# Decode block on one core: the second MLP layer with batches on four column groups, folded into rows of 512 bytes, and a first MLP layer that finishes eight column tiles early

## The chip, the core and the metric

The kernel runs on one core of a Trainium2 chip. The metric is the device time of one execution in microseconds (us). Times within the profile ("at 663.3") count from the first instruction; the span from the first to the last instruction is some 1.7 to 1.8 us shorter than the device time.

In the profile's lines PE is TensorE's matmuls, PEld its weight loads, DVE VectorE, ACT ScalarE, SPq and ACTq the issue of a transfer by the sync and the scalar engine. A transfer has *landed* when the last of its completions is counted. A *column group* is 32 of the array's 128 columns, worked as a small array of its own.

## The reference

One decode step of a block with adaptive layer norm: modulation from `c`, cached attention over 8192 keys, then an MLP with squared ReLU. What matters here is its last line and the MLP:

```python
# B = 8 batches, D = 512, F = 1792; k_cache and v_cache are (8, 8, 8192, 128) bf16
mod = silu(c) @ w_mod                       # six vectors of 512 per batch
x = x + ga * attention(h, k_cache, v_cache, wq, wo)
h = layernorm(x) * (1 + cb) + sb
r = maximum(h @ w1 + b1, 0)
x = x + gb * ((r * r) @ w2 + b2)            # the part that the change rewrites
```

## The kernel before

Nearly everything is loaded through one queue, the sync engine's: `w_mod`, `wq`, then 64 units of keys and values of 4 MB each through four ring slots, and at the very end, in the ring slot that came free, W1 in two pieces and W2 in four:

```python
d_w1 = [dma("sync", s_w1[i], ...W1v[:, a:z]...) for i, (a, z) in enumerate(((0, 3), (3, 4)))]
d_w2 = [dma("sync", s_w2[i], ...W2v[:, a:z, :]...)
        for i, (a, z, j) in enumerate(((0, 4, 4), (4, 8, 4), (8, 12, 4), (12, 14, 2)))]
```

The MLP keeps hidden units on partitions and the 8 batches in the columns. The first layer walks k outermost over all 14 column tiles, so no tile is complete before the last k. The second layer loads each 128x128 block of W2 as the stationary operand and streams 8 columns. Its result has the output features on partitions, so it must be transposed through TensorE before it can be stored:

```python
for f in range(FT):                          # FT = 14 row tiles of W2
    for k in range(KT):                      # KT = 4 column blocks
        t = op("tensor", lambda e: e.matmul(yT_ps[:, k, :], W2v[:, f, k*128:(k+1)*128], hidT[:, f, :],
               ...), [k_sq[f // 8], d_w2[f // 4]])      # waits for the piece of W2
...                                          # residual x1T transposed into o_ps (L778)
k_y2 = op("vector", ... y2T = yT_ps * mod(5))           # L781
for cc in (1, 0):
    ...                                      # y2T transposed into o_ps (L786)
    # copy o_ps to SBUF on ScalarE (cc = 1) or VectorE (cc = 0), then store 8 rows of 512 bytes
```

Of the kernel before, what the change touches and what calls it, by code (L numbers as in the profile page):

```python
# [5 lines left out]
ACT = mybir.ActivationFunctionType  # L6
ALU = mybir.AluOpType
# [161 lines left out]
def bass_adaLN_cond__gqa_block_cached__dense_activation_squared_relu__decode_kernel(  # L169
# [17 lines left out]
    with ExitStack() as es:  # L187
# [25 lines left out]
        SEL = sb("SEL", [128, 4, 8], BF16)  # L213
# [13 lines left out]
        SELB = sb("SELB", [4, 4, B], BF16)  # L227
        SELP = sb("SELP", [128, B], FP32)
        x1T = sb("x1T", [128, KT, B], BF16)
# [4 lines left out]

        KF = KTb[:, :, :, :].rearrange("p a t r -> p (a t r)")
# [10 lines left out]
        EYEB = KF[:, 4544:4576].rearrange("p (g b) -> p g b", g=4)  # L246
# [5 lines left out]
        hidT = KF[:, 2560:2560 + FT * B].rearrange("p (f b) -> p f b", f=FT)  # L252
        out_sb = KF[:, 2048:2304]
# [4 lines left out]
        y2T = KF[:, 0:KT * B].rearrange("p (k b) -> p k b", k=KT)  # L258
# [34 lines left out]
        def pool(fn, deps=()):  # L293
            return op("gpsimd", fn, deps)

        pool(lambda e: e.memset(IDENT[:], 0.0))
        pool(lambda e: e.memset(IDF8[:], 0.0))
# [4 lines left out]
        pool(lambda e: e.memset(R4m[:], 0.0))  # L302
        pool(lambda e: e.memset(SEL[:], 0.0))
# [6 lines left out]
        def select(ap, pattern, base, cm, fill, cmp, dep):  # L310
            return pool(lambda e: e.affine_select(ap, ap, pattern=pattern, compare_op=cmp, fill=fill,
                                                  base=base, channel_multiplier=cm), [dep])
# [3 lines left out]
        t = select(IDF8[:], [[-1, 8]], 0, 1, 1.0, NE, t)  # L316
        k_id = t
        pool(lambda e: e.memset(KF[:, 4096:4096 + 64 * KT], 0.0))
        pool(lambda e: e.memset(EYE[:], 0.0))
        t = pool(lambda e: e.memset(EYEB[:], 0.0))  # L320
        t = select(EYE[:], [[-32, 4], [-1, B]], 0, 1, 1.0, NE, t)
        t = k_eye = select(EYEB[:], [[-32, 4], [-1, B]], 0, 1, 1.0, NE, t)
# [3 lines left out]
        for d in (-96, -64, -32, 0, 32, 64, 96):  # L326
            t = select(R4[:], [[-1, 128]], -d, 1, 1.0, NE, t)
        t = select(Qmask[:], [[-32, 4]], 0, 1, 0.0, GE, t)
        t = select(Qmask[:], [[32, 4]], 31, -1, 0.0, GE, t)
        for d in (0, 32, 64, 96):  # L330
            t = select(R4m[:], [[-1, 32]], -d, 1, 0.5, NE, t)

        for i in range(4):
            for cg in range(4):
                for half in range(2):
                    t = select(SEL[:, i, 4 * half:4 * half + 4], [[-1, 4]], -(32 * cg + 8 * i + 4 * half), 1,
                               1.0, NE, t)
# [5 lines left out]
        t = select(SELB[:], [[-1, 4], [0, B]], 0, 1, 1.0, NE, t)  # L343
# [89 lines left out]
        for u in range(2):  # L433
            for i in range(4):
                t = op("tensor", lambda e, u=u, i=i: e.matmul(
                    QT_ps[:, u, :, i, :], q_r[:, u, DH * i:DH * (i + 1)], EYEB[:, :, :]), [k_q[u]])
# [12 lines left out]
        k_cb1 = op("vector", lambda e: e.tensor_scalar(cb1[:], mod(4), 1.0, None, ALU.add))  # L449

# [8 lines left out]
        d_bb = dma("sync", s_bb, lambda e: e.dma_start(b2_row, B_b2.rearrange("(o f) -> o f", o=4)))  # L459
# [57 lines left out]
        yT_ps = bank(2)[:, 0:KT * B].rearrange("p (k b) -> p k b", k=KT)  # L517
# [31 lines left out]
        for b in range(B):  # L549
# [76 lines left out]
            for p in range(NP):  # L626
# [22 lines left out]
                if not lastu:  # L649
# [9 lines left out]
                    for i in range(4):  # L659
                        t = op("tensor", lambda e, i=i, osb=osb, oT_ps=oT_ps: e.matmul(  # L660
                            oT_ps, osb[:, i * 128:(i + 1) * 128], SEL[:, i, :], start=(i == 0), stop=(i == 3)),
                            [k_osb, k_all])
                        if i == 0:
                            released[n % NSLOT] = t
                            if n + NSLOT < len(units):
                                load(n + NSLOT)
# [7 lines left out]
                else:  # L674
# [29 lines left out]
                    for hh, (f0, n, a, z) in enumerate(((0, 4, 0, 2), (0, 4, 2, 3), (4, 2, 3, 4))):  # L704
                        for j in range(n):
                            op("tensor", lambda e, hh=min(hh, 1), f0=f0 + j, j=j, n=n, a=a, z=z: e.matmul(
                                hT_ps[hh][:, f0:f0 + 4 * (z - a - 1) + 1:4, 1, :], brow(j, n), SELB[:, a:z, :],
                                start=(f0 == 0), stop=False, skip_group_check=True), [d_bb, s_bank_free[min(hh, 1)]])
                    op("tensor", lambda e: e.matmul(
                        yT_ps, b2_row, SELB[:, :, :], start=True, stop=False, skip_group_check=True),  # L710
# [6 lines left out]
                    for i in range(4):  # L717
                        op("tensor", lambda e, i=i: e.matmul(
                            oT_ps, osb[:, i * 128:(i + 1) * 128], SEL[:, i, :], start=False, stop=False,
                            skip_group_check=True), [t, k_all])  # L720
# [16 lines left out]
        k_x1 = op("vector", lambda e: e.tensor_tensor(x1T[:], t1T[:], xT[:], ALU.add), [t])  # L737
        mean_ps = bank(3)[:, 0:B]
        for k in range(KT):
            t = op("tensor", lambda e, k=k: e.matmul(mean_ps, ONESMB[:, :], x1T[:, k, :], start=(k == 0),  # L740
                                                    stop=(k == KT - 1)), [k_x1])
        bc = lambda ap: ap.unsqueeze(1).to_broadcast([128, KT, B])
        t = op("vector", lambda e: e.tensor_tensor(xcT[:], x1T[:], bc(mean_ps), ALU.subtract), [t])
# [8 lines left out]
        for k in range(KT):  # L752
            if k == KT - 1:
                t = op("tensor", lambda e: e.matmul(var_ps, ONESM[:, :], sqs[:]), [k_sqs])
                t = op("scalar", lambda e: e.activation(std2[:], var_ps, ACT.Sqrt, bias=epst[:, 0:1]), [t])
                k_rstd = op("vector", lambda e: e.reciprocal(rstd2[:], std2[:]), [t])
            for f in range(FT):
                t = op("tensor", lambda e, f=f, k=k: e.matmul(
                    hT_ps[f // 8][:, f % 8, :, :], wcol(k, f), hbT[:, k, :, :], start=False, stop=(k == KT - 1),
                    skip_group_check=True), [k_hb, k_sb, d_w1[k // (KT - 1)]])  # L760
                if k == KT - 1 and f in (7, FT - 1):
                    hh = f // 8
                    fs = slice(8 * hh, f + 1)
                    t = op("vector", lambda e, hh=hh, fs=fs: e.tensor_tensor(
                        rT[:, fs, :], hT_ps[hh][:, :, 0, :], rsb(fs.stop - fs.start), ALU.mult), [t, k_rstd])
                    t = op("vector", lambda e, hh=hh, fs=fs: e.tensor_tensor(
                        rT[:, fs, :], rT[:, fs, :], hT_ps[hh][:, :, 1, :], ALU.add), [t])
                    k_sq.append(op("vector", lambda e, fs=fs: e.scalar_tensor_tensor(
                        hidT[:, fs, :], rT[:, fs, :], 0.0, rT[:, fs, :], ALU.max, ALU.mult), [t]))
        o_ps = bank(4)[:, 0:256]  # L770
        for f in range(FT):
            for k in range(KT):
                t = op("tensor", lambda e, f=f, k=k: e.matmul(  # L773
                    yT_ps[:, k, :], W2v[:, f, k * 128:(k + 1) * 128], hidT[:, f, :],
                    start=False, stop=(f == FT - 1), skip_group_check=True), [k_sq[f // 8], d_w2[f // 4]])
        for cc in range(2):
            for k in range(2):
                op("tensor", lambda e, k=k, cc=cc: e.matmul(  # L778
                    o_ps[64 * cc:64 * cc + B, 128 * k:128 * (k + 1)], x1T[:, 2 * cc + k, :], IDENT[:, :],
                    start=(k == 0), stop=False, tile_position=(0, 64 * cc), skip_group_check=True), [k_x1])  # L780
        k_y2 = op("vector", lambda e: e.tensor_tensor(y2T, yT_ps, mod(5), ALU.mult), [t])  # L781
        outf = out.rearrange("b s d -> (b s) d")
        d_o = []
        for cc in (1, 0):
            for k in range(2):
                t = op("tensor", lambda e, k=k, cc=cc: e.matmul(  # L786
                    o_ps[64 * cc:64 * cc + B, 128 * k:128 * (k + 1)], y2T[:, 2 * cc + k, :], IDENT[:, :],
                    start=False, stop=(k == 1), tile_position=(0, 64 * cc), skip_group_check=True), [k_y2])
            rows = slice(64 * cc, 64 * cc + B)
            if cc == 0:  # L790
                t = op("vector", lambda e, rows=rows: e.tensor_copy(out_sb[rows, :], o_ps[rows, :]), [t])
            else:
                t = op("scalar", lambda e, rows=rows: e.activation(out_sb[rows, :], o_ps[rows, :], ACT.Copy), [t])
            d_o.append(dma(("sync", "scalar")[cc], s_out[cc], lambda e, cc=cc, rows=rows: e.dma_start(
                outf[:, 256 * cc:256 * (cc + 1)], out_sb[rows, :]), [t]))
# [32 lines left out]
```

## Time and profile before

| | before |
|---|---|
| time, median of 3 | 668.38 us (668.37 to 668.46) |
| span in the profile | 666.7 us |
| moved by the 16 DMA engines | 283.85 MB at 426 GB/s |
| TensorE / VectorE / ScalarE busy | 79% / 46% / 40% |
| granted TensorE clock from 658 us on | 0.50 |

The busy shares say little: TensorE is busy 79% of the span, and yet the DMA engines are above 90% busy in every slice but the last, so there is little to win before the last few microseconds. The reader has to look at the tail by itself. Here are the two output issues, from the timeline of the kernel before (start, length, engine):

```profile
664.85 0.30 ACTq L794 DMA_DIRECT2D out_dram<-KTb  x1
664.92 0.31 SPq L794 DMA_DIRECT2D out_dram<-KTb  x1
```

### The profile page before, as it was taken

To read this page: it belongs to the slowest core of one execution; us is meant where nothing else is said; L and a number is where in the kernel's file an instruction comes from. 1 tells how busy PE (TensorE), PEld (TensorE's weight loads), DVE (VectorE), ACT (ScalarE), POOL (GpSimd) and SP (SyncE) were. 2 spreads that over 40 slices of the span, in tenths; PEclk is the share of its full clock that TensorE was granted. 3 is DMA by queue.
4 is the path that set the end of the run, shared out by engine and by line. 5 is a ranking of instruction groups with operands and counts; after the bars stand their busy time and mean duration, and the time that the engine had idled before them with its cause. 6 is when DMAs were issued, how large, how long until landed. Compare 5 with 4: busy or idle time off the path is not lost.

```text
span 666.7 us, 15924 instructions
## 1 busy us (share of the span) xinstructions
PE 528.3 (79%) x7259; PEld 352.2 (53%) x7259; DVE 307.9 (46%) x587; ACT 264.3 (40%) x307; POOL 20.5 (3%) x79
## 2 busy tenths in 40 slices
PE   3494976898849987599858988499776998589887
PEld 2383732675328742477316753287424773277535
DVE  1262741466316652367415662167513673146633
ACT  2151631466115651166314661166512663146611
POOL 7400000000000000000000000000000000000000
PEclk9696998799969999699998999799997999879996
DMA  9999999999999999999999999999999999999997
GB/s 375 437 406 441 419 433 433 425 434 431 438 427 433 433 434 427 434 434 425 434 431 438 427 431 434 434 427 431 438 425 434 433 436 427 431 434 434 427 420 285
DMA packets 12189, 283.85 MB, mean 426 GB/s; under 512 B 1261, under 2 KB 1297, under 8 KB 3601
## 3 DMA queue, kind: packets, MB, share of 16 engines
q1 hardware_dynamic: 12128, 283.65, 99.3%
q8 instruction: 9, 0.15, 0.1%
q10 hardware_dynamic: 48, 0.02, 0.0%
q14 instruction: 4, 0.02, 0.0%
HBM read 283.66 MB, written 0.01 MB: 425 GB/s over the span
## 4 chain that ended last, share of the span: by engine, by line
PE 52%; DMA 38%; ACT 6%; DVE 2%; issue 1%; SPq 0%; DVEq 0%
PE PS L488 36%; DMA ring<-in_A_k_cache_dram 33%; PE PS L505 9%; ACT P_sb L582 5%; DMA ring<-in_A_v_cache_dram 4%; DMA ring<-in_A_wq_dram 2%; PE PS L636 2%; PE PS L478 1%; ACT KTb L493 1%; DVE O_sb L656 1%; PE PS L472 1%; PE PS L594 1%; DVE Pm L608 0%; PE PS L614 0%; PE PS L773 0%
## 5 line engine op out<-in xcount | busy, mean ns | idle before, releaser
L488 PE MATMUL PS<-IDENT,ring 128*128 128x128 bf16 x4096 | 267.1, 227 | 56.2 <-DMA ring<-in_A_k_cache_dram 56.2
L488 PEld LDWEIGHTS PS<-IDENT,ring 128*128 128x128 bf16 x4096 | 246.5, 102 | 104.8 <-DMA ring<-in_A_k_cache_dram 57.4
L493 ACT ACTIVATE KTb<-PS 128x1024 bf16<-128x1024 bf16 x192 | 196.5, 1024 | 236.6 <-PE PS L488 236.6
L495 DVE COPY KTb<-PS 128x1024 bf16<-128x1024 bf16 x320 | 210.0, 688 | 146.5 <-PE PS L488 144.4
L636 PE MATMUL PS<-ring,Pm 128*32 128x512 bf16 x1018 | 67.2, 409 | 24.8 <-DMA ring<-in_A_v_cache_dram 23.9
L505 PE MATMUL PS<-KTb,Qb 128*32 128x512 bf16 x1024 | 79.0, 385 | 4.5 <-ACT KTb L493 4.5
L656 DVE CAST O_sb<-PS 128x512 bf16<-128x512 f32 x31 | 21.5, 692 | 112.7 <-PE PS L636 112.7
L636 PEld LDWEIGHTS PS<-ring,Pm 128*32 128x32 bf16 x1018 | 26.5, 101 | 61.8 <-DMA ring<-in_A_v_cache_dram 33.7
L535 ACT ACTIVATE KTb<-PS 32x192 bf16<-32x192 f32 (+1 forms) x18 | 5.6, 310 | 110.0 <-PE PS L472 103.9
L582 ACT ACTIVATE P_sb<-PS,negm 128x1024 bf16<-128x1024 f32 x32 | 35.2, 1111 | 20.2 <-DVE negm L577 20.2
L478 PE MATMUL PS<-ONES 128*128 128x512 f32 x80 | 42.1, 630 | 0.0
L472 PE MATMUL PS<-IDENT 128*128 128x512 bf16 x112 | 33.4, 380 | 0.0
L594 PE MATMUL PS<-IDENT,P_sb 128*128 128x128 bf16 x256 | 19.9, 220 | 15.4 <-ACT P_sb L582 15.4
L608 DVE COPY Pm<-PS 64x512 bf16<-64x512 bf16 x48 | 20.2, 421 | 25.0 <-PE PS L594 24.5
L594 PEld LDWEIGHTS PS<-IDENT,P_sb 128*128 128x128 bf16 x256 | 14.4, 98 | 25.1 <-ACT P_sb L582 25.1
L505 PEld LDWEIGHTS PS<-KTb,Qb 128*32 128x32 bf16 x1024 | 15.4, 94 | 21.0 <-ACT KTb L493 8.5
L512 DVE TENSOR_REDUCE m<-PS 128x1 f32<-128x512 f32 x32 | 22.1, 689 | 6.6 <-PE PS L505 6.6
L660 PEld LDWEIGHTS PS<-SEL,O_sb 128*128 128x128 bf16 x124 | 5.8, 97 | 30.0 <-DVE O_sb L656 30.0
L478 PEld LDWEIGHTS PS<-ONES 128*128 128x128 f32 x80 | 12.7, 190 | 10.6 <-issue 10.6
L660 PE MATMUL PS<-SEL,O_sb 128*128 128x8 bf16 x124 | 7.8, 169 | 12.3 <-DVE O_sb L656 12.0
L472 PEld LDWEIGHTS PS<-IDENT 128*128 128x128 bf16 x112 | 9.9, 104 | 10.1 <-issue 7.2
L543 PE MATMUL PS<-wo_sb,KTb 128*32 128x512 bf16 x192 | 11.8, 380 | 3.3 <-ACT KTb L535 3.3
(134 smaller groups left out, 147.0 us busy)
## 6 DMA issues: line engine op xcount, KB each, us to landing
ring<-in_A_k_cache_dram SPq DMA_DIRECT2D x32, 4096.0 KB, 34.0
ring<-in_A_v_cache_dram SPq DMA_DIRECT2D x31, 4096.0 KB, 27.8
ring<-in_A_wq_dram SPq DMA_DIRECT2D x1, 4096.0 KB, 19.8
wo_sb<-in_A_wo_dram SPq DMA_DIRECT2D x1, 4096.0 KB, 47.3
ring<-in_w_mod_dram SPq DMA_DIRECT2D x1, 3072.0 KB, 10.5
ring<-in_A_v_cache_dram SPq DMA_DIRECT2D x1, 2048.0 KB, 22.5
ring<-in_B_w_dram SPq DMA_DIRECT2D x3, 512.0 KB, 19.2
ring<-in_B_w_dram SPq DMA_DIRECT2D x1, 1344.0 KB, 17.8
```

The source lines that it names most:

```text
L472: ts = [op("tensor", lambda e: e.matmul(bank(at).rearrange("p (a r) -> p a r", a=4), IDENT[:, :], rhs)) for _ in range(n)]
L478: ts = [op("tensor", lambda e: e.matmul(bank(at).rearrange("p (a r) -> p a r", a=4), ONES[:, :], rhs)) for _ in range(n)]
L488: t = op("tensor", lambda e, j=j, i=i: e.matmul(STG[j][:, i, :], src[:, 32 * k + 8 * j + i, :], IDENT[:, :], is_transpose=True), [loaded[n ...
L493: stg_free[j] = op("scalar", lambda e, j=j, dst=dst: e.activation(dst, STG[j], ACT.Copy), [t])
L495: stg_free[j] = op("vector", lambda e, j=j, dst=dst: e.tensor_copy(dst, STG[j]), [t])
L505: t = op("tensor", lambda e, hf=hf, q=q, rhs=rhs: e.matmul(PS[32 * q:32 * (q + 1), k, :], Qb[:, 2 * p + hf, :], rhs, start=(p == 0 and hf ...
L512: return op("vector", lambda e: e.tensor_reduce(m4[:, k:k + 1], bank(k), AX.X, ALU.max), [t])
L582: exps.append(op("scalar", lambda e, k=k: e.activation(P_sb[:, k, :, :, :], bank(k).rearrange("p (i x) -> p i x", i=8).unsqueeze(2).to_bro ...
L594: t = op("tensor", lambda e, k=k, i=i: e.matmul(STG[k][:, i, :], P_sb[:, k, i, :, :].rearrange("p h x -> p (h x)"), IDENT[:, :], is_transp ...
L608: done.append(op("vector", lambda e, dst=dst, frm=frm: e.tensor_copy(dst, frm), [t, k_pm]))
L636: t = op("tensor", lambda e, m=m, cg=cg, p=p, vt=vt, Obank=Obank: e.matmul(Obank[32 * cg:32 * (cg + 1), :], lhs[:, p, 32 * m:32 * m + 32], ...
L656: t = op("vector", lambda e, osb=osb, Obank=Obank: e.tensor_copy(osb, Obank), [t])
```

## The change

Its intent is to shorten that tail in three places. The first layer runs column tiles 0 to 7 for all four k before tiles 8 to 13, so that eight tiles of the hidden layer are ready early, and the variance matmul moves forward with it. The second layer puts the batches (8, padded to 32) into the stationary operand and streams 128 columns of W2, on four column groups of the array at once. Its result then has batches on partitions and needs no transpose: one multiply by the gate, two adds that fold 128 partitions into 64, and the store. The core of the diff:

```diff
-        for k in range(KT):
-            if k == KT - 1: ... variance, sqrt, reciprocal
-            for f in range(FT): ... first layer
+        for hh, (fa, fz) in enumerate(((0, 8), (8, FT))):
+            for k in range(KT):
+                if (hh, k) == (0, 2): ... variance, sqrt, reciprocal
+                for f in range(fa, fz): ... first layer
...
         for f in range(FT):
             for k in range(KT):
-                    yT_ps[:, k, :], W2v[:, f, k * 128:(k + 1) * 128], hidT[:, f, :],
+                    y_ps[32 * k:32 * (k + 1), :], hidw[:, f, :], W2v[:, f, 128 * BLK[k]:128 * (BLK[k] + 1)],
+                    ... tile_position=(0, 32 * k)
...
-        k_y2 = ... y2T = yT_ps * mod(5);  transposes of x1T and y2T into o_ps;  two copies
+        t = op("vector", lambda e: e.tensor_tensor(y_sb, y_ps, mod5[:], ALU.mult), [t])
+        for h in range(2):
+            rows = slice(64 * h, 64 * (h + 1))
+            t2 = op("vector", lambda e, h=h, rows=rows: e.tensor_tensor(
+                out_sb[:, h, :], y_sb[rows, :], x1_sb[rows, :], ALU.add), [t, k_res])
```

The rest prepares this: `hidw` and `x1w` are zero-padded to 32 columns, `mod5` holds the gate in the new layout, x1 is brought into it early (L739, L769).

## The prediction

> **What bounds the kernel now.** I read the page first: the slices and the chain.
>
> ```profile
> span 666.7 us, 15924 instructions
> ...
> DMA  9999999999999999999999999999999999999997
> ...
> q1 hardware_dynamic: 12128, 283.65, 99.3%
> ```
>
> The 16 DMA engines are above 90% busy in every slice but the last. What they move (283.65 MB in that queue) is untouched by the change, so at most the last slice or so can be won. That is the tail: the second MLP half and the output, after the last values have landed. The chain of waits in order of time, cut to that stretch (start, length, what):
>
> ```profile
> 658.28 1.53 PE PS L758 x42
> 659.80 0.44 PE PS L754 x2
> 660.25 0.02 issue
> 660.27 0.28 ACT std L755
> ...
> 661.40 0.24 DVE KTb L768
> 661.64 0.04 issue
> 661.68 1.02 PE PS L773 x32
> 662.70 0.13 issue
> 662.83 0.92 PE PS L773 x24
> 663.75 0.31 PE PS L778 x4
> 664.06 0.40 PE PS L786 x4
> 664.46 0.02 issue
> 664.49 0.41 DVE KTb L791
> ```
>
> On the face of it this is compute from end to end: the first layer (L758), the variance (L754, L755), three VectorE steps, the second layer (L773, 56 matmuls), transposes, a copy, the output transfer. But between the 32nd and the 33rd matmul of L773 stands a 0.13 us "issue", a wait that the chain cannot name. The 33rd is the first one that reads the third piece of W2, which arrives in four pieces (row tiles 0-3, 4-7, 8-11, 12-13). So I asked for the issue times of the third and fourth piece (the sync queue's timeline, narrowed to each) and for their time to landing (the DMA view, narrowed the same way):
>
> ```profile
> 647.88 1.94 SPq L682 DMA_DIRECT2D ring<-in_B_w_dram  x1
> 649.87 0.89 SPq L682 DMA_DIRECT2D ring<-in_B_w_dram  x1
> ring<-in_B_w_dram SPq DMA_DIRECT2D x1, 512.0 KB, 14.8
> ring<-in_B_w_dram SPq DMA_DIRECT2D x1, 256.0 KB, 13.5
> ```
>
> Third piece: 647.88 + 14.8 = 662.7 us. Fourth: 649.87 + 13.5 = 663.4 us. The 33rd matmul starts at 662.83, just after the third landing. Stretches of the second layer's line say the same of the fourth (columns: stretch, length, PE busy and count, weight loads, granted clock, DMA share, GB/s):
>
> ```profile
> 662.80:663.25 0.45, 0.42 (x16) 0.45 (x16) 0.50 0.01 5
> 663.25:663.36 0.11, 0.11 (x6) 0.06 (x3) 0.50 0.00 0
> 663.36:663.60 0.24, 0.24 (x10) 0.23 (x8) 0.50 0.00 0
> ```
>
> The eight weight loads of the last two row tiles all lie after 663.36, when the fourth piece is there. **The tail is therefore bound by the arrival of W2 until about 663.37 us**, and by compute only from there to 666.7: 3.3 us.
>
> **What the Trainium skill says.** "TensorE: Matmul & The Clock Gate", Part 1, "What's actually happening": an idle TensorE falls back to half its clock. The trace agrees: granted clock 0.50 in the rows above. "TensorEngine Tiling (Array Packing)", "Restrictions" and "Key Properties": column tiling switches fast weight load off, and a change of tiling mode drains the array; but different tiles run in parallel. The trace agrees with the parallel part: 32 values matmuls of 32 columns by 512 (L636) take 1.91 us, 60 ns apart, while one lasts 380 ns. No row gives the drain's price. "VectorE: DVE Perf Modes", "The perf-mode tier table": a two-tensor operation on bf16 in SBUF reaches 2x, with a PSUM or fp32 operand 1x; no row of the kernel before shows the 2x case.
>
> **The change part by part.**
>
> *Prologue.* GpSimd loses 32 selects for SEL (6.0 us busy), three of seven for R4 and all four for R4m, and gains two memsets. Its chain before ended at 29.4 us while the first key block landed only at 30.8, so nothing waits for it that does not wait longer for a transfer. Four 32x128 VectorE copies (mod5) come in, some 0.2 us each by the 32-column SBUF rows plus 0.1 (estimate 0.3); they fall into the 2.89 us that VectorE idles before L552. Worth 0.
>
> *First layer.* It now runs tiles 0-7 for all four k, then 8-13. The variance matmul goes in after 16 instead of 42 matmuls. At (1.53-0.18)/41 = 33 ns each, that is 26 x 33 = 0.86 us earlier; the sums it needs are ready at 658.57 and it would start at 658.28 + 16 x 0.033 = 658.81. Reciprocal, three VectorE steps and the second layer's start move with it: 661.68 - 0.86 = about 660.8. Four residual matmuls (L739) fit into the half microsecond in which PE waits for L743 and L745.
>
> *Second layer, until its last piece.* By 660.8 only the first W2 piece is there. Row tiles 8-11 still cannot start before 662.7, nor 12-13 before 663.37. **So the 0.86 us is spent waiting for W2: worth 0.** The last eight matmuls: before, 663.37 to 663.75, after which VectorE starts L781 at 663.78. After, they are two rounds of four column groups with 128 moving columns. At half clock a round streams in about 107 ns (a round of four took 512 columns in 4 x 60 = 240 ns at full clock; a quarter of the columns at half the clock is 120 ns) and a cold matmul on 128 columns lasts 0.27 to 0.31 us (L778, mean 292 ns). 663.37 + 0.11 + 0.31 = 663.79. VectorE starts at about 663.81: lost 0.03.
>
> *Behind it.* Before: L781 0.19, transposes L786 0.38, copy L791 0.41 with hand-overs: 663.78 to the later output issue at 664.92, 1.14 us. After: one 128x128 multiply out of PSUM (L427, a copy of that shape, took 292 ns), hand-over 0.03, two adds of 128 columns in SBUF, the second starting 0.14 to 0.21 after the first, lasting 0.22 (2x) to 0.28 (1x: 184 ns for 32 columns plus 96/0.96 ns), hand-over 0.03. Sum 0.29 + 0.03 + 0.14 + 0.22 + 0.03 = 0.71, or 0.84 at 1x. Gain 0.30 to 0.43. The x1 copy (L769) runs at about 661.4, in VectorE's idle time. The output transfers are again two of 8 rows of 512 bytes, so their 1.78 us stay.
>
> Sum: 0.36 (middle) - 0.03 = **0.33 us**; 668.38 - 0.33 = **668.05 us**.
>
> **Rivals.** *All the compute in the chain counts.* Then 0.86 from the order, some 0.25 from the packed matmuls and 0.36 at the end come off: 1.5 us, 666.9. For it: the chain names PE almost throughout. Against it: the two landings, 662.7 and 663.4, each met by a start just behind it. *The narrow column groups cost more than counted* (slow weight loads, a drain, slow adds across partitions): 0.3 us or more on the end path takes the gain back, 668.3 to 668.5. For it: no 128-column matmul in column groups is in the trace; against it, only eight of the 56 are exposed. *The transfer stream shifts*: different GpSimd and issue order in the prologue could move every transfer a little. Against it: over 10 MB are queued by then and the queue never runs dry.
>
> **Range and chances.** The end path gives 0 to 0.5 us; run to run the kernel before spread 0.09 us, and another session may add a few tenths. 667.5 to 668.6 should hold it. A change of 2% is 13 us, more than the whole stretch touched: within 2% is all but certain.
>
> **What would show each step.** Right: the first matmul of L772 near 660.8, then gaps in it; its last eight loads still after about 663.3; the first VectorE multiply (L776) at 663.8; output issue at 664.5 to 664.65; span about 666.35. The skill's 2x for the adds: under 0.23 us each. Wrong: last eight loads well before 663.3 (then W2's arrival was not the bound), or L776 later than 664.0 (then column groups cost more), or a DMA view with another total or landing times moved by more than 0.3 us.

## The result and the profile after

The changed kernel took 668.47 us (median of 4, 668.33 to 669.83), the kernel before, in the same rounds and earlier ones, 668.42 us. The ratio is 1.0002, 95% interval 0.9985 to 1.0019: the same.

The chain of waits of the changed kernel, its end:

```profile
647.97 14.79 DMA ring<-in_B_w_dram
662.76 0.14 issue
662.89 0.98 PE PS L772 x20
663.88 0.02 issue
663.90 0.30 DVE KTb L776
664.20 0.02 issue
664.23 0.22 DVE KTb L779
664.44 0.23 DVEq L787
```

Before, the 32nd matmul ended at 662.70 and W2's third piece landed at 662.69, all but level, and the nameless 0.13 us followed. Now the same nameless 0.14 us has the transfer in front of it: the chain runs back from the second layer straight into the transfer of W2's third piece, issued at 647.97 and landed 14.79 us later. Nothing of the first layer, the variance or the hidden layer stands in it any more. The timeline shows why:

```profile
660.90 1.30 PE L772 MATMUL PS<-ring,hidw 128*32 128x128 bf16 x32 [0.17 <-DVE hidw L767]
...
662.89 0.95 PE L772 MATMUL PS<-ring,hidw 128*32 128x128 bf16 x24 [0.69 <-DMA ring<-in_B_w_dram]
663.44 0.14 PEld L772 LDWEIGHTS PS<-ring,hidw 128*32 128x32 bf16 x8 [0.19 <-DMA ring<-in_B_w_dram]
663.90 0.29 DVE L776 TENSOR_TENSOR KTb<-PS,mod 128x128 bf16<-128x128 f32 x1 [2.25 <-PE PS L772]
664.23 0.45 DVE L779 TENSOR_TENSOR KTb<-KTb 64x128 bf16<-64x128 bf16 x2
664.70 0.32 SPq L782 DMA_DIRECT2D out_dram<-KTb  x1
664.71 0.31 ACTq L782 DMA_DIRECT2D out_dram<-KTb  x1
```

The second layer starts at 660.90 instead of 661.68. Then it stands: the idle time in brackets (how long before, and what ended it) is now DMA, 0.69 us before the third piece and 0.19 us of the weight loader before the fourth. The last eight weight loads begin at 663.44. Before, they began after 663.36. The fourth piece itself, from the sync queue's timeline and the DMA view narrowed to its issue:

```profile
649.96 0.88 SPq L677 DMA_DIRECT2D ring<-in_B_w_dram  x1
ring<-in_B_w_dram SPq DMA_DIRECT2D x1, 256.0 KB, 13.4
```

So it landed at 649.96 + 13.4 = 663.4, by the semaphore records at 663.398; before, at 663.326. The gain in front of it was waited away; what is left is the stretch behind it. By the records of the two traces:

| us | before | after |
|---|---|---|
| fourth piece of W2 landed, at | 663.33 | 663.40 |
| from there to the first VectorE operation of the end | 0.46 | 0.50 |
| from there to the later output issue | 1.14 | 0.81 |
| from there to the end of the span | 1.80 | 1.90 |
| landing to end, sum | 3.40 | 3.21 |
| span | 666.73 | 666.61 |

The end of the path became 0.20 us shorter, and in this pair of traces 0.07 us of it went into a later landing.

### The profile page after: what moved, and what is told of

Read it like the earlier page. It is cut to its first block, busy times and chain, and to the rows that moved or that the text cites. A ratio compares the mean times of both kernels' runs of the same rounds, so it can differ in the third digit from the quotient of the medians.

```text
span 666.6 us, 15837 instructions
## 1 busy us (share of the span) xinstructions
PE 528.3 (79%) x7255; PEld 353.7 (53%) x7255; DVE 309.2 (46%) x593; ACT 264.1 (40%) x306; POOL 13.5 (2%) x37
## 4 chain that ended last, share of the span: by engine, by line
PE 52%; DMA 36%; ACT 7%; DVE 2%; SPq 1%; issue 1%; DVEq 0%
PE PS L483 37%; DMA ring<-in_A_k_cache_dram 32%; PE PS L500 9%; ACT P_sb L577 5%; PE PS L631 2%; DMA ring<-in_B_w_dram 2%; DMA ring<-in_A_wq_dram 2%; PE PS L473 1%; ACT KTb L488 1%; SPq L677 1%; DVE O_sb L651 1%; PE PS L467 1%; PE PS L589 1%; DVE Pm L603 1%; PE PS L609 0%
## 5 line engine op out<-in xcount | busy, mean ns | idle before, releaser
L631 PE MATMUL PS<-ring,Pm 128*32 128x512 bf16 x1018 | 64.4, 395 | 23.5 <-DMA ring<-in_A_v_cache_dram 22.6
L655 PEld LDWEIGHTS PS<-R,O_sb 128*128 128x128 bf16 x124 | 5.8, 97 | 29.5 <-DVE O_sb L651 29.4
L655 PE MATMUL PS<-R,O_sb 128*128 128x8 bf16 x124 | 7.9, 169 | 12.3 <-DVE O_sb L651 12.0
```

The source lines that it names most:

```text
L631: t = op("tensor", lambda e, m=m, cg=cg, p=p, vt=vt, Obank=Obank: e.matmul(Obank[32 * cg:32 * (cg + 1), :], lhs[:, p, 32 * m:32 * m + 32], ...
```

## The experiments

**Theory A:** the arrival of W2's last pieces sets the second layer's end, so only what lies behind it counts. **Rival B:** compute sets it, the first layer's new order did give its 0.86 us, and something else in the change (narrow column groups, adds across partitions) took it back. Each experiment says in numbers what either expects.

### e1: the changed kernel with the first layer's old order

```diff
-        for hh, (fa, fz) in enumerate(((0, 8), (8, FT))):
-            for k in range(KT): ...
+        for k in range(KT):
+            if k == KT - 1: ... variance
+            for f in range(FT): ...          # as in the kernel before
```

> The changed kernel with the first layer's old order (all 14 column tiles for each k). Theory A (the arrival of W2 sets the second layer's end): the second layer starts about 0.86 us later, near 661.75 instead of 660.90, but its last eight weight loads still come right after the fourth piece of W2 at about 663.4; time within 0.15 us of the changed kernel, 668.4. Rival B (the compute chain sets the end, and the new order gave 0.86 us that something else took back): 669.2 to 669.3.

Measured: 668.35 us (median of 4), ratio to before 0.9995 (0.9976 to 1.0014). The second layer starts 0.85 us later than in the changed kernel and its end hardly moves. Timeline:

```profile
661.75 2.14 PE L773 MATMUL PS<-ring,hidw 128*32 128x128 bf16 x56 [1.00 <-DVE hidw L768]
...
663.48 0.14 PEld L773 LDWEIGHTS PS<-ring,hidw 128*32 128x32 bf16 x8 [0.19 <-DMA ring<-in_B_w_dram]
663.94 0.29 DVE L777 TENSOR_TENSOR KTb<-PS,mod 128x128 bf16<-128x128 f32 x1 [1.45 <-PE PS L773]
```

The last eight weight loads come at 663.48, still released by the transfer, against 663.44. B's 669.2 did not come. The order is worth nothing here that the times show.

### e8: the kernel before with the first layer's new order

```diff
-        for k in range(KT): ...              # 14 tiles for each k
+        for hh, (fa, fz) in enumerate(((0, 8), (8, FT))): ...
```

> The kernel before with the first layer's new order alone. A (the arrival of W2 sets the second layer's end): the second layer starts 0.86 us earlier, near 660.9, and its last eight matmuls still come right behind the fourth piece, so the time of the kernel before within 0.15 us. B (compute sets it): 667.5.

Measured: 668.39 us (median of 5) beside 668.40 for the kernel before, ratio 0.9998 (0.9986 to 1.0011). The timeline shows the mirror of e1: the second layer of full 128-column weights now starts at 660.68, and waits.

```profile
660.68 1.28 PE L772 MATMUL PS<-KTb,ring 128*128 128x8 bf16 x32 [0.17 <-DVE KTb L767]
...
662.70 0.92 PE L772 MATMUL PS<-KTb,ring 128*128 128x8 bf16 x24 [0.74 <-DMA ring<-in_B_w_dram]
```

With old and new second layer alike, the early start turns into 0.7 us of waiting for the third piece.

### e2 and e3: take the late pieces of W2 away

Only the first piece of W2 is loaded and stands in for all row tiles. The result is wrong (relative error 0.105); the number and shape of all matmuls stay.

```diff
-  for i, (a, z, j) in enumerate(((0, 4, 4), (4, 8, 4), (8, 12, 4), (12, 14, 2)))]
+  for i, (a, z, j) in enumerate(((0, 4, 4),))]
-  W2v[:, f, ...] ... d_w2[f // 4]
+  W2v[:, f % 4, ...] ... d_w2[0]
```

> The kernel before, with only the first of the four pieces of W2 loaded and read for all row tiles (wrong result on purpose). A: the second layer runs without gaps, 56 x 26.7 ns + 0.17 from 661.68 to about 663.35 instead of 663.75; time 668.0, 0.4 us less than before. B: no wait on W2 is there to be removed, 668.4.

> The changed kernel with only the first of the four pieces of W2 loaded and read for all row tiles (wrong result on purpose). A: without W2's late pieces the earlier start of the second layer counts: 14 groups x 0.107 us + 0.31 from 660.90 to about 662.7 instead of 663.85; time about 667.3, some 1.1 us less than the changed kernel and 0.7 to 0.9 us less than the kernel before with the same edit. B: the same as before with the same edit, within 0.2 us.

Measured: the kernel before so cut took 667.96 us, the changed kernel so cut 667.02 us, medians of 4 beside 668.54 for the kernel before; the four runs of one (667.74 to 668.24) do not overlap with those of the other (666.87 to 667.30). (e2's profiled run had its attention values landed about 0.5 us earlier than the others, so its single instants are not compared with theirs.) With the wait gone, **the change is worth 0.94 us**; with it, nothing that the times show. This is the plainest sign of A: the same two kernels differ or not according to whether W2 is late. B, which expected no difference between the two, is out.

The two runs measure something else by the way, the second layer without a wait. The rows of its matmuls (count, then busy time and mean ns of one, then idle time before), e2 first:

```profile
L773 PE MATMUL PS<-KTb,ring 128*128 128x8 bf16 x56 | 1.7, 168 | 1.0 <-DVE KTb L768 1.0
```

```profile
L772 PE MATMUL PS<-ring,hidw 128*32 128x128 bf16 x56 | 1.7, 312 | 0.2 <-DVE hidw L767 0.2
```

and the stretch of each (PE busy, weight loads busy, granted clock, DMA share, GB/s):

```profile
661.30:663.10 1.80, 1.65 (x56) 1.57 (x56) 0.50 0.00 0
```

```profile
660.90:662.80 1.90, 1.68 (x56) 1.42 (x56) 0.50 0.00 0
```

56 matmuls took 1.65 us with full weights and 1.68 us on four column groups. The ends of matmuls are modelled in the profile, but the start of the VectorE operation that waits for the last one says the same: 1.69 us after the first matmul in e2, 1.74 us in e3. At half clock the packing bought no time in the second layer, where the prediction's first rival had some 0.25 us. From the first matmul to the end of the span are 4.64 us in e2 and 4.45 in e3, so some 0.2 of the 0.94 us come from the shorter end and the rest from the earlier start.

### e4: make W2 later

One more transfer of 512 KB is put between the third and the fourth piece.

```diff
+  d_ext = dma("sync", s_ext, lambda e: e.dma_start(
+      RING[:, s0, KT * F + FT * D:KT * F + FT * D + 4 * D], B_w2[0:512].rearrange("(p j) n -> p (j n)", p=128, j=4)))
   d_w2.append(w2p(3, 12, 14, 2))
```

> The changed kernel with one more transfer of 512 KB between the third and the fourth piece of W2. A: the fourth piece lands 1.25 us later (the spacing of the 512 KB pieces), about 664.65, and the whole time follows: about 669.7. B: the extra transfer hides behind compute, less than 0.3 us.

Measured: 670.58 us (median of 4), ratio 1.0027 (1.0009 to 1.0045), more than A expected. The fourth piece, issued at 650.75, landed 14.6 us later, at 665.36: the extra transfer pushed it by 1.96 us, not by 1.25. The first of its 16 completions came 1.33 us later than in the changed kernel, the 15th 1.68, so the DMA engines drifted further apart; why was not followed up. The whole end moved with it:

```profile
665.40 0.41 PE L777 MATMUL PS<-ring,hidw 128*32 128x128 bf16 x8 [1.97 <-DMA ring<-in_B_w_dram]
665.86 0.29 DVE L781 TENSOR_TENSOR KTb<-PS,mod 128x128 bf16<-128x128 f32 x1 [4.11 <-PE PS L777]
```

From landing to VectorE are again 0.50 us, and the span rose by 1.94 us (666.61 to 668.55) for a landing 1.96 us later; the medians of the times are 2.1 us apart. The wait passes one for one into the time, as A says; the size that A was given for the transfer was wrong.

### e5: which part of the transfer is late

The landing of a piece is the last of 16 completions, one of each DMA engine. For the fourth piece they are spread over 1.9 to 2.2 us in the traces (2.8 in e4), and the last is 0.2 to 0.7 us behind the one before it (0.8 in e4); the 2.2 and 0.5 us of the expectation below are those of the changed kernel and e1, not of the kernel before (2.0 and 0.37). Behind the fourth piece, 16 tiny transfers of 1 to 16 rows were queued.

```diff
+  d_ext = [dma("sync", s_ext[n], ...RING[0:n + 1, s0, ...] <- B_w2[0:n + 1, 0:64]) for n in range(16)]
```

> The changed kernel with 16 tiny transfers behind the fourth piece of W2, of 1, 2, ... 16 rows of 128 bytes, each with its own semaphore. In the traces so far the 16 completions of one piece of W2 are 2.2 us apart, the last one alone 0.5 us behind the rest. If a transfer of n rows runs on n DMA engines, the smaller ones land at different times, between about 661.3 and 663.6 us, and each that lands later than the one before it names an engine that lags. If rows are spread over all engines, all land together at about 663.5. The output comes up to 0.5 us later than in the changed kernel if the queue's issues are in its way, otherwise as there.

Measured (one look, its state unknown): 668.41 us. The fourth piece's completions run from 661.34 to 663.51, the last two at 663.24 and 663.51. The transfer of six rows landed at 662.96, that of seven rows at 663.72. The Trainium skill, "DMA: Bandwidth & Descriptors", "Why a DMA increments its semaphore by 16 and not by 1", says that such a transfer of n rows (up to 16) runs on the n lowest-numbered engines. The trace agrees that it uses n of them: each transfer of n rows shows n late completions. Read with that page, the seventh engine is the one that lags in this run: within the transfer of seven rows the last completion comes 0.56 us after the sixth (663.16). Each tiny transfer also cost every engine that it used about 0.2 us: the first engine's completions come at 661.90, 662.08, 662.25, 662.44. So the wait for the fourth piece, landed at 663.51, was a wait for the slowest of 16 engines. No version that shifts rows to other engines was built; what makes that engine lag stays open.

### e6 and e9: the changed kernel again, in more rounds

> The changed kernel itself, unedited, in more rounds beside the kernel before, to see whether the 0.2 us that the traces show behind the landing of W2's fourth piece (before 3.40 us from landing to end, after 3.21) are there in the times. Expected 0.1 to 0.3 us less than before, 668.2 to 668.4 where before has 668.4 to 668.5; a rival is that the landing itself moves by as much from run to run and nothing can be told.

> The changed kernel, unedited, on the same chip as the two above. Expected 0.2 us less than the kernel before and 0.15 to 0.2 us more than e7_gate_last, in the medians; the intervals of the ratios will be wider than that because some runs of every kernel are 1 to 1.5 us longer.

Measured: e6 668.15 us (median of 5: 668.13 to 668.33 and one of 669.85) beside 668.57, ratio 0.9993 (0.9980 to 1.0007). e9 668.38 us (median of 5, 668.14 to 668.48) beside 668.40, ratio 0.9996 (0.9983 to 1.0009). The rival in e6's expectation is the truer one: the stretch behind the landing hardly differs between traces with the same end, but the landing moves by up to 0.3 us from run to run, so the times alone do not show the 0.2 us. Of e9's expectation the 0.2 us to e7 came (668.38 to 668.17), the 0.2 us to the kernel before did not (0.02).

| us, from the traces | landing of the fourth piece, at | landing to VectorE | to output issue | to end | sum |
|---|---|---|---|---|---|
| before | 663.33 | 0.46 | 1.14 | 1.80 | 3.40 |
| e8, before with new order | 663.20 | 0.46 | 1.14 | 1.81 | 3.41 |
| after | 663.40 | 0.50 | 0.81 | 1.90 | 3.21 |
| e6, after again | 663.20 | 0.50 | 0.81 | 1.90 | 3.21 |
| e9, after again | 663.48 | 0.50 | 0.81 | 1.90 | 3.20 |
| e1, after with old order | 663.44 | 0.50 | 0.81 | 1.87 | 3.17 |
| e4, W2 late | 665.36 | 0.50 | 0.81 | 1.88 | 3.19 |
| e5, probe | 663.51 | 0.50 | 0.81 | 1.86 | 3.17 |
| e7, gate last | 663.19 | 0.50 | 0.62 | 1.90 | 3.03 |

### e7: shorten what lies behind the landing

If only the end path counts, work should be moved off it into the wait for W2. Here the residual is divided by the gate (with 1e-20 in place of a gate of zero) and accumulated in PSUM before the third piece, so that the gate's multiply comes last and writes the folded rows itself.

```diff
+        rg5 = 1 / mod5                       # in the prologue, where VectorE idles
-        k_res = ... x1_sb = x1_ps
+        k_res = ... x1_sb = x1_ps * rg5
+            if f == 8: ... e.matmul(y_ps, IDENT[:, :], x1_sb, start=False, stop=False)
-        y_sb = y_ps * mod5;  out_sb[:, h, :] = y_sb[rows, :] + x1_sb[rows, :]
+        out_sb[:, h, :] = y_ps[rows, :] * mod5[rows, :]
```

> The changed kernel with the residual divided by the gate and accumulated in PSUM while PE waits for W2's third piece, so that behind the last matmuls stand two multiplies of 64x128 out of PSUM and no adds. If only what lies behind the landing of W2's fourth piece counts: 0.29 + 0.29 + 0.05 us of VectorE in place of 0.81, so 0.15 to 0.2 us less than the changed kernel, 667.95 to 668.2. If that path does not set the end, the time of the changed kernel. Its output should be correct; the residual is rounded to bf16 once more.

Measured: correct. Median of 6 runs 668.17 us (668.40 for the kernel before, 668.38 for e9 on the same chip), with four runs from 667.91 to 668.40 and two of 669.46 and 669.77; those two make the ratio 1.0002 (0.9990 to 1.0014), so by the times nothing is proved. The timeline has what was meant:

```profile
663.69 0.59 DVE L785 TENSOR_TENSOR KTb<-PS,mod 64x128 bf16<-64x128 f32 x2 [2.25 <-PE PS L779]
664.31 0.32 SPq L788 DMA_DIRECT2D out_dram<-KTb  x1
```

From landing to end it needs 3.03 us, 0.18 less than the changed kernel and 0.38 less than the kernel before. Its three lowest runs, 667.91, 667.93 and 667.94, are the lowest of any kernel here with a correct result. It is the best end path, worth some tenths of a microsecond in 668, and not separated from the others by its interval.

## Why the prediction was right, point by point

- **The bound.** Right: the last eight weight loads after W2's fourth piece, at 663.44 where "after about 663.3" was forecast. e1, e8, e2 with e3, and e4 each show it from another side. The half clock that the working uses is in every trace (0.50 from 656 to 658 us on). What brought it is not shown: in the kernel before TensorE was busy 7.2 of the 8.2 us ahead of the change at 656.2.
- **Prologue, worth 0.** The part seen fits: the four gate copies took 0.92 us from 26.71 us on, where VectorE had idled before (2.89 us in front of L552). It was not tested by itself.
- **First layer, 0.86 us earlier and worth 0.** Right: start at 660.90 (forecast 660.8), 0.78 us before the old start, and no time from it in e1 and e8.
- **Second layer until VectorE, 0.03 lost.** Landing to VectorE grew from 0.46 to 0.50 us, so 0.04. The absolute 663.81 became 663.90, 0.07 of which is the later landing. Of the two figures for a round, 107 and 120 ns, the first is right: e3's rounds start 107 ns apart. (The 240 ns behind the second counts the tail of the last matmul; in the kernel before, L636's rounds start about 215 ns apart, and a quarter of that at half the clock is again 107 ns.)
- **Behind it, 0.30 to 0.43 gained.** Measured 1.143 - 0.809 = 0.33, within the range. One term was off inside it. The multiply took 292 ns as forecast. Each add took 218 to 221 ns, the faster of the two cases: the Trainium skill, "VectorE: DVE Perf Modes", "The perf-mode tier table", is borne out, since e7's multiplies of the same shape out of PSUM took 283 and 293 ns. But the second add started 0.23 us after the first, not 0.14: it began 13 ns after the first had ended. The operations that started 0.14 us apart (L768 and the next L764, before) overlapped by 83 ns; both begin at partition 0, the two adds at partitions 0 and 64. The four gate copies (L442), which write from partitions 0, 32, 64 and 96 on, also start 13 to 14 ns after the one before has ended, as do e7's two multiplies. That the starting partition decides is therefore likely; no run moved it alone.
- **Output, "their 1.78 us stay".** This is the term that failed. From the later issue to the end there were 1.80 to 1.81 us before, in e8 and in e2, and 1.86 to 1.90 us in the eight traces with the new end. Most of it lies in the stores themselves: from the later issue to the last completion 1.35 us with the old end, 1.41 to 1.48 with the new, and from there to the end of the span 0.46 with the old, 0.41 to 0.46 with the new. Before, the two issues were 79 ns apart, and the first store's rows had gone out (until 665.72) when the second's began (665.74); after, they were 4 ns apart, and the rows of both went out between 665.49 and 665.68. That they get in each other's way is likely, but no run spaced them, and the stores also read other partitions than before.
- **Sum.** 0.33 - 0.09 - 0.04 = 0.20 us in place of 0.33, 0.19 to 0.24 over the traces (3.40 and 3.41 against 3.17 to 3.21). It is too little for the times: the landing of W2 alone moves by 0.3 us between runs of one kernel. The forecast of 668.05 was therefore 0.4 us too low, near none of the changed kernel's first four runs. Of the signs named in advance, the output issue came at 664.71 and not by 664.65, and the span was 666.61, not 666.35. The range of 667.5 to 668.6 also holds the time of the kernel before, so hitting it says little; what bears the prediction out is the wait, seen in the traces and tested by taking W2 away.
- **The rivals.** All the compute in the chain counts: refuted by e1 and e8. Narrow column groups cost 0.3 us or more on the end path: refuted by 0.50 against 0.46 us. The stream shifts: it does, by tenths, but in every kernel.

## What to carry to other kernels

In a kernel that the transfers fill, find for each stage of the tail when its last operand lands, and count only work behind that instant; work in front of it can be made faster without end and buys waiting. A short "issue" without a name between two matmuls of one line is worth a look at landing times. Where a transfer is last, move work off the path behind it, and test such a claim by taking the transfer away in both versions: 0.94 us of difference without it, none that could be measured with it.

## What the Trainium skill lacked or had wrong

- "TensorEngine Tiling (Array Packing)", "Theoretical Speedup", names up to 4 times for a small dimension of at most 32. Here, at half clock, 56 matmuls on four column groups with 128 moving columns took 1.68 us, and the same work with full weights and 8 moving columns 1.65 us. The page lists this use (operands swapped, with column tiling) but gives no time for it beside the plain form.
- "DMA: Bandwidth & Descriptors", "Latency and other measured facts", names engines 7 and 15 as usually slow. Read with that page's rule for few rows, the seventh engine (number 6) lagged in e5: 662.96 us for six rows, 663.72 for seven. The page says that the engines finish independently, but not by how much: the fourth piece's completions were 1.9 to 2.2 us apart here.
- "VectorE: DVE Perf Modes", "Two Vector instructions with no wait between them", has a model by which an instruction that starts in another group of 32 partitions is held until the earlier ones have finished, but gives no time for it. The second add fits: it started 13 ns after the end of the first (0.23 us after its start), where pairs that start at the same partition overlapped by some 80 ns.
- "DMA: Bandwidth & Descriptors", "Issuing engines are not separate DMA queues", says that transfers of different issuers interleave on the same DMA engines; it does not tell what two small stores issued at once cost each other: 1.86 to 1.90 us from issue to end when issued 4 ns apart, 1.80 at 79 ns. The cause is not shown.
